# Exponentials in three groups a batch, weight chunks rounded earlier and a busier start, in a fused attention and SwiGLU kernel

## The chip, the cores and the metric

One NeuronCore of a Trainium2 chip runs the whole kernel. The metric is the device time of one execution in microseconds (us), read from several executions. The engines are TensorE (PE, matmuls; PEld is its weight load), VectorE (DVE), ScalarE (ACT), GpSimd (POOL) and SyncE (SP, which issues DMAs). The kernel gives each engine its own list of instructions; where one needs another's result, it waits for a semaphore.

## The reference

```python
# x: (4, 12416, 128), inducing: (32, 128); weights of the FFN are float64
def mab(q, kv):
    s = (q @ kv.transpose(0, 2, 1)) / sqrt(128)
    a = exp(s - s.max(-1, keepdims=True))
    return (a / (a.sum(-1, keepdims=True) + 1e-09)) @ kv
h = mab(inducing, x)            # 32 rows a batch: first softmax, over 12416 columns
y = mab(x, h)                   # second softmax, over 32 columns
xn = y / sqrt(mean(y * y) + 1e-06) * rms_g
g, val = xn @ w_gate, xn @ w_val         # 128 -> 1536
out = (g / (1 + exp(-g)) * val) @ w_out  # silu(g) * val, 1536 -> 128
```

## The kernel before

The FFN is a stream of 1,200 **slots**: 4 batches of 25 units of tokens, each with 12 slots of 128 hidden columns. In a slot PE makes gate and value, ACT makes silu, DVE multiplies the two into `u`, and PE multiplies some earlier `u` by `w_out`. Most of these output products are "plain" (fp32). Some are "split" into three fp32r matmuls, whose operands ACT and POOL make first; `ready` is the slot from which a split product may be issued.

```python
def slot(j, products, steps):
    g = ps_gv.tile([P, 512], F32, name="gv", tag="gv")     # ps_gv: four PSUM banks in turn
    nc.tensor.matmul(g[:, 0:T], sg[:, ts(j, P)], a[:, 0:T], start=True, stop=True)
    sl = silp.tile([P, 512], F32, name="silu")
    nc.scalar.activation(sl[:, 0:T], g[:, 0:T], AF.Silu)
    products()                                             # one or two earlier output products
    v = ps_gv.tile([P, 512], F32, name="gv", tag="gv")
    nc.tensor.matmul(v[:, 0:T], sv[:, ts(j, P)], a[:, 0:T], start=True, stop=True)
    t = up.tile([P, 512], F32, name="u")
    nc.vector.tensor_tensor(out=t[:, 0:T], in0=sl[:, 0:T], in1=v[:, 0:T], op=ALU.mult)
    steps()                                                # this slot's share of the attention
    # ... (u joins the plain or the split products that wait)
```

The attention of the next batch is dealt out over the slots by `steps()`. Its two softmaxes have seven **batches of exponentials** in the stream: one of batch 0 (its second softmax), then two for each later batch. Each is one long instruction on ACT (in batch 0 and in the second softmax a short one follows). A `mark` is its slot. Ahead of a mark, `products()` holds products back, so that PE has a stock of five (`LAG`) to live on:

```python
add(254, g["exp2"], 0, NS)          # in schedule(b)
marks += [134, 254]                 # 134: exp1, the first softmax
# ...
hold = any(k < e <= k + 3 for e in marks)   # in products(), k is the slot
if hold and count < LAG:
    return
```

Two other parts matter. First, x's phase and the start, before slot 0: x comes in seven blocks, PE turns each and makes the scores, then come the first softmax, its sums (`sum_h`), h, and the first tokens' RMS norm. `warm(n)` issues n matmuls whose result nobody reads. Second, the **rounding**: the weights come as float64, in nine chunks, and each is rounded to fp32 from its bits by some seven instructions on DVE, ACT and POOL (`power`, `power_number`, `upper`, `upper_number`, `sign`, `lower`). The early chunks are done before slot 0, the rest in slots 0 to 16, where the stream already needs them.

Last, a **seam** turns one group of attention weights into the FFN's input: transposes on DVE, a power of -0.5 on POOL (`scale`, 2.9 us), its application (`apply`) on POOL, another DVE transpose (`turn_b`), `split`.

Of the kernel before, what the change touches and what calls it, by code (L numbers as in the profile page):

```python
# [18 lines left out]
P = 128  # L19
R = 4  # L20
# [4 lines left out]
def kernel(  # L25
# [109 lines left out]
    def load_rows(b, s):  # L135

        n = per[s]
        t = xnat[b, s] = xnp.tile([P, 16 if b and n > 4 else n, C], F32, name=f"xn{s % 2 if b and n > 4 else s}")
        if b or s == full:
            for q in range(R):  # L140
                nc.sync.dma_start(out=t[ts(q, m), 0:n, :], in_=of(xrows, b, s)[q])
        else:
            d = xrows[ds(start[s], P * n), :].rearrange("(p t) c -> p t c", t=n)
            for t0, t1 in (((0, R), (R, 2 * R), (2 * R, n)) if not s else ((0, n),)):
                nc.sync.dma_start(out=t[:, t0:t1, :], in_=d[:, t0:t1, :])
# [43 lines left out]

    warm(4)  # L190
    ps = ps_m.tile([P, 512], F32, name="mm", tag="mm")
# [27 lines left out]
    def rounding(i, c):  # L219
# [19 lines left out]

        def power(engine=nc.scalar):  # L240
            if i < 2:
                t = w0[i, c] = (silp.tile([P, 512], F32, name="silu") if (i, c) == (1, 0) else
                                 third.tile([P, 512], F32, name="hs") if (i, c) == (1, 1) else
                                 wp.tile([P, 512], F32, name="w"))
                dst = st["dst"] = t[:]
            else:
                dst = st["dst"] = wo.rearrange("p j c -> p (j c)")[:, ts(c, 512)]
            if not wide:
                nc.sync.dma_start(out=dst if i < 2 else dst.rearrange("p (j c) -> p j c", c=C), in_=source(i, c))
                return  # L250
            words = raw[i, c].rearrange("p (f w) -> p f w", w=2)
            st["low"], st["high"] = words[:, :, 0], words[:, :, 1]
            e = st["e"] = work.tile([P, 512], I32, name="we", tag="work")
            nc.vector.tensor_scalar(out=e[:], in0=st["high"], scalar1=20, scalar2=0x7FF,
                                    op0=ALU.logical_shift_right, op1=ALU.bitwise_and)
            if engine is not nc.scalar:
                nc.vector.tensor_scalar(out=e[:], in0=e[:], scalar1=896.0, scalar2=1151.0, op0=ALU.max, op1=ALU.min)

        def power_number(engine=nc.scalar):
            if wide:  # L260
                numbers("e", -896.0 * (1 << 23), float(1 << 23), engine)

# [29 lines left out]
    def attention(b, load_next):  # L292
# [56 lines left out]
        def max3():  # L349
# [4 lines left out]
            nc.vector.tensor_copy(out=nbias[:], in_=ps[:, 0:1])  # L354

        def exp1():
            hl = st["hl"] = once.tile([P, C + 1], F32, name="hl")
            part = sc[b][:, 0:SC1]
            nc.scalar.activation(part, part, AF.Exp, bias=st["nbias"][:], scale=SCALE, accum_out=hl[:, C:C + 1])

# [233 lines left out]
    def ffn(b, u):  # L594
# [59 lines left out]

        def slot(j, products, steps):
            g = ps_gv.tile([P, 512], F32, name="gv", tag="gv")
            nc.tensor.matmul(g[:, 0:T], sg[:, ts(j, P)], a[:, 0:T], start=True, stop=True)  # L657
            sl = silp.tile([P, 512], F32, name="silu")
            nc.scalar.activation(sl[:, 0:T], g[:, 0:T], AF.Silu)  # L659
            products()  # L660
            v = ps_gv.tile([P, 512], F32, name="gv", tag="gv")
            nc.tensor.matmul(v[:, 0:T], sv[:, ts(j, P)], a[:, 0:T], start=True, stop=True)  # L662
            t = up.tile([P, 512], F32, name="u")
            nc.vector.tensor_tensor(out=t[:, 0:T], in0=sl[:, 0:T], in1=v[:, 0:T], op=ALU.mult)  # L664
            steps()
# [10 lines left out]
    for s in range(NS):  # L676
        load_rows(0, s)
        for _ in range(1 if s == 1 else 4 if s == NS - 1 else 0):
            fetch_raw(*unread.pop(0))
    weight = {one: rounding(*one) for one in chunks}  # L680

    def parts(i, c, *engine):
        one = weight[i, c]
        one["power"](*engine)
        one["power_number"](*engine)
        one["upper"]()
        one["upper_number"](*engine)
# [6 lines left out]
    for s in range(NS):  # L694
        for k in range(R):
            f["turn_x"](s, k)
        if s:
            f["scores1"](s - 1)
        if s == 2:
            parts(0, 0, nc.vector)  # L700
        if s == 3:
            join(0, 0)
    f["scores1"](NS - 1)
    f["max1"]()
    warm(4)
    f["max2"]()
    warm(3)
    f["max3"]()
    warm(8)
    f["exp1_of"](0, 1)  # L710
    for s in range(NS):
        if s % 2:
            f["exp1_of"](s, min(s + 2, NS))
        f["turn_e"](s)
        if s == 5:
            parts(1, 0)
        if s == NS - 1:
            f["fold_l"]()
        f["sum_h"](s)
# [3 lines left out]
    f["square_h"]()  # L723
    weight[1, 0]["sign"]()
    f["stack_of"](0, 0)
    warm(10)
    f["scores2"](0, ps)
    f["sub_max"](0)
    weight[1, 0]["lower"]()
    f["exp2"](0, 1)  # L730
# [4 lines left out]
    square()  # L735
    parts(2, 0)
    f["stack_of"](1, 0)
    warm(26)
    turn_z()
    scale()  # L740
    weight[2, 0]["sign"]()
    for i in range(2):
        f["stack_low"](i, 0)
    parts(0, 1)
    apply()
    turn_b()
    split()
    weight[2, 0]["lower"]()
    spread(0, 0)
    warm(3)  # L750
    gather(0, 1)
    gather(0, 2)
    join(0, 1)
    flowing.append(True)
# [5 lines left out]
    def schedule(b):  # L760
# [4 lines left out]
        def add(k, step, *args):  # L765
            plan.setdefault(int(k), []).append(lambda: step(*args))
            if getattr(step, "__name__", "") == "sub_max" and args[0]:
                busy[int(k)] = 1.1

        if not b:  # L770
            for k, one in ((0, (1, 1)), (3, (2, 1)), (7, (0, 2)), (10, (1, 2)), (13, (2, 2))):
                for j, name in ((0, "power"), (1, "power_number"), (1, "upper"), (2, "upper_number"), (2, "sign"), (3, "lower")):
                    add(k + j, weight[one][name])
            for k, *one in ((2, 0, 1), (5, 1, 1), (12, 0, 2), (15, 1, 2)):
                add(k, f["stack_of"], *one)
# [3 lines left out]
            for s in range(1, NS):  # L779
                add(2 * s + 16, f["scores2"], s)  # L780
                add(2 * s + 17, f["sub_max"], s)
            add(3 * NS + 9, f["exp2"], 1, NS)
            marks.append(3 * NS + 9)
        if b + 1 < B:
# [4 lines left out]
            for s in range(NS):  # L789
# [8 lines left out]
                add(203 + 7 * s, g["sub_max"], s)  # L798
            for k, name in ((126, "max1"), (128, "max2"), (130, "max3"), (134, "exp1"), (187, "fold_l"), (189, "divide"), (191, "turn_h"),
                            (193, "square_h")):  # L800
                add(k, g[name])
            for i in range(2):
                add(175 + 23 * i, g["fetch"], i)
                add(197 + 7 * i, g["stack"], i)
                for k in range(R):
                    add(199 + 7 * i + k, g["place"], i, k)
            add(254, g["exp2"], 0, NS)
            marks += [134, 254]
        if b + 2 < B:
# [8 lines left out]
    for k, (b, s) in enumerate(order):  # L818
# [5 lines left out]
        for late_by, one in enumerate(following):  # L824
            for i, step in enumerate(seam(*one)):
# [3 lines left out]
                seams.setdefault(at, []).append(step)  # L829
                seam_busy[at] = seam_busy.get(at, 0) + {3: 3.0, 4: 1.2, 6: 1.4}.get(i, 0)  # L830
    flat = [(b, u) for b in range(B) for u in range(NU)]
    after = dict(zip(flat, flat[1:]))
# [18 lines left out]
    for b in range(B):  # L851
# [6 lines left out]
        for k, (u, j) in enumerate(order):  # L858
# [16 lines left out]
            def products():  # L875
# [3 lines left out]
                count = max(len(plain) - 1, 0) + sum(at <= now for at, _ in kara)  # L879
                hold = any(k < e <= k + 3 for e in marks)  # L880
                if hold and count < LAG:
# [8 lines left out]
            if u not in unit:  # L890
                unit[u] = ffn(b, u)
            unit[u](j, products, steps)
    while kara or plain:
# [33 lines left out]
```

## Time and profile before

| | before |
|---|---|
| time, median of 4 runs | 1690.6 us (1689.47 to 1691.07) |
| start of slot 0 | 55.42 us |
| PE busy share; PE's share of the chain that ended last | 98%; 90% |
| half clock inside the stream | 54.8 to 58.2 us, 126.5 to 129.9 us |
| ACT table loads | 16, of 1.28 us |

PE is nearly always busy, so time can only be won where PE waits, runs at half clock, or does filler. This is the timeline of before around one such wait (start, duration, engine, line, operation, operands; in brackets the idle time just before and what ended it):

```profile
119.72 2.90 POOL L524 TENSOR_TENSOR rs<-ms,mhalf 128x16 f32<-128x16 f32 x1 [0.19 <-DVE ms L522]
...
122.70 1.05 POOL L528 TENSOR_TENSOR sc<-sc,rs 128x512 f32<-128x512 f32 x1
123.70 1.27 POOL L650 TENSOR_TENSOR xn<-hs,u 128x512 fp32r<-128x512 f32 x1
...
125.03 0.50 PE L607 MATMUL acc<-xn,xn 128*128 128x512 f32 x1 [2.68 <-POOL xn L650]
```

The reader is to see a queue on POOL: the power of the first seam, its application, and only then L650, the last step of a split product's operand. PE stands still for 2.68 us until that operand is there.

### The profile page before, as it was taken

What the parts mean: (1) busy time and instruction counts of PE and PEld (TensorE: products, weight loads), DVE (VectorE), ACT (ScalarE), POOL (GpSimd) and SP (SyncE); (2) the same over time, 40 slices, a digit from 0 to 9 for tenths busy, and PEclk for the clock granted to TensorE, in tenths of its full rate; (3) what the DMA queues carried; (4) which work ended last, traced back from release to release, by engine and by line L of the source; (5) the groups of instructions that cost most, each with busy time, mean ns of one, the idle gap of its engine ahead of it and who ended that gap; (6) DMA issues with size and microseconds to landing.
All of it is one profiled execution on the core that took longest, in us unless ns stands there. A gap on an engine that the chain in (4) does not pass through costs nothing.

```text
span 1688.5 us, 23205 instructions
## 1 busy us (share of the span) xinstructions
PE 1660.7 (98%) x6756; PEld 1036.6 (61%) x6756; DVE 1166.2 (69%) x1941; ACT 1237.4 (73%) x2216; POOL 1159.4 (69%) x931
## 2 busy tenths in 40 slices
PE   9989999999999999999999999999999999999998
PEld 6546665655676565665566666565557666666666
DVE  4877775676667776667667777676767666666665
ACT  4547777766787777776778777777677888788786
POOL 0336775777587775776668777577657888888884
PEclk9999999999999999999999999999999999999999
DMA  6445523433444131524335314252211111111111
GB/s 233 106 64 90 86 57 83 101 85 59 68 81 68 37 82 30 124 60 102 60 64 83 58 33 82 51 131 65 50 30 38 30 39 32 38 32 38 31 36 26
DMA packets 389454, 112.38 MB, mean 67 GB/s; under 512 B 365104, under 2 KB 369744, under 8 KB 386896
## 3 DMA queue, kind: packets, MB, share of 16 engines
q1 hardware_dynamic: 389136, 110.89, 32.1%
q8 instruction: 54, 0.88, 0.2%
q14 instruction: 72, 0.59, 0.1%
q10 hardware_dynamic: 192, 0.02, 0.0%
HBM read 53.95 MB, written 27.00 MB: 48 GB/s over the span
## 4 chain that ended last, share of the span: by engine, by line
PE 90%; ACT 2%; issue 1%; POOL 1%; DVE 1%; DVEq 0%; POOLq 0%; ACTq 0%
PE acc L607 42%; PE gv L657 17%; PE gv L662 16%; PE u L625 5%; PE u L623 5%; PE mm L330 3%; PE mm L509 1%; PE mm L388 1%; DVE u L664 1%; ACT silu L659 1%; ACT L659 1%; PE mm L461 0%; ACT L448 0%; POOL xn L650 0%; ACT sc L448 0%
## 5 line engine op out<-in xcount | busy, mean ns | idle before, releaser
L664 DVE TENSOR_TENSOR u<-silu,gv 128x512 f32<-128x512 f32 (+2 forms) x1200 | 788.0, 664 | 470.8 <-PE gv L662 236.0
L659 ACT ACTIVATE silu<-gv 128x512 f32<-128x512 f32 (+2 forms) x1200 | 698.6, 584 | 376.4 <-PE gv L657 340.0
L607 PE MATMUL acc<-u,wo 128*128 128x512 f32 (+2 forms) x1600 | 794.1, 580 | 3.5 <-DVE u L664 2.2
L662 PE MATMUL gv<-a,sv 128*128 128x512 f32 (+2 forms) x1188 | 760.2, 640 | 0.9 <-DVE u L664 0.6
L645 POOL TENSOR_TENSOR xn<-u,xn 128x512 fp32r<-128x512 f32 (+2 forms) x400 | 503.4, 1258 | 366.8 <-ACT xn L644 329.3
L650 POOL TENSOR_TENSOR xn<-hs,u 128x512 fp32r<-128x512 f32 (+2 forms) x400 | 503.6, 1259 | 39.3 <-ACT hs L649 36.1
L657 PE MATMUL gv<-a,sg 128*128 128x512 f32 (+2 forms) x1188 | 486.2, 409 | 6.0 <-ACT silu L659 6.0
L657 PEld LDWEIGHTS gv<-a,sg 128*128 128x128 f32 x1188 | 224.9, 189 | 238.3 <-ACT silu L659 120.6
L607 PEld LDWEIGHTS acc<-u,wo 128*128 128x128 f32 x1600 | 298.6, 189 | 82.6 <-issue 16.4
L662 PEld LDWEIGHTS gv<-a,sv 128*128 128x128 f32 x1188 | 224.7, 189 | 194.5 <-issue 137.7
L644 ACT ACTIVATE xn<-u 128x512 fp32r<-128x512 f32 (+2 forms) x400 | 247.7, 619 | 25.6 <-DVE u L664 23.7
L649 ACT ACTIVATE hs<-xn 128x512 f32<-128x512 f32 (+2 forms) x400 | 245.8, 614 | 4.9 <-POOL xn L650 4.0
L607 PE MATMUL acc<-xn,xn 128*128 128x512 f32 (+2 forms) x400 | 156.5, 391 | 4.5 <-POOL xn L650 4.5
L625 PE MATMUL u<-xn,xn 128*128 128x512 f32 (+2 forms) x400 | 155.7, 389 | 0.0
L623 PE MATMUL u<-xn,xn 128*128 128x512 f32 (+2 forms) x400 | 155.3, 388 | 0.0
L607 PEld LDWEIGHTS acc<-xn,xn 128*128 128x128 f32 x400 | 75.0, 188 | 24.2 <-POOL xn L650 7.6
L524 POOL TENSOR_TENSOR rs<-ms,mhalf 128x16 f32<-128x16 f32 (+2 forms) x28 | 75.9, 2709 | 16.9 <-DVE ms L522 15.1
L625 PEld LDWEIGHTS u<-xn,xn 128*128 128x128 f32 x400 | 75.2, 188 | 18.1
L623 PEld LDWEIGHTS u<-xn,xn 128*128 128x128 f32 x400 | 75.1, 188 | 16.8 <-issue 0.7
L616 DVE STREAM_TRANSPOSE o<-o 128x512 f32<-128x512 f32 (+2 forms) x97 | 67.7, 698 | 3.4
L615 DVE TENSOR_TENSOR o<-acc,o 128x512 f32<-128x512 f32 (+2 forms) x97 | 64.9, 669 | 0.0
L628 ACT ACTIVATE o<-u 128x512 f32<-128x512 f32 (+2 forms) x97 | 56.4, 582 | 0.0
(165 smaller groups left out, 745.1 us busy)
## 6 DMA issues: line engine op xcount, KB each, us to landing
out_dram<-o SPq DMA_DIRECT2D x320, 64.0 KB, 1.9
xn<-in_x_dram SPq DMA_DIRECT2D x62, 256.0 KB, 4.8
xT<-in_x_dram SPq DMA_DIRECT2D x60, 256.0 KB, 5.4
a<-hi SPq DMA_DIRECT2D x156, 64.0 KB, 2.0
a<-lo SPq DMA_DIRECT2D x156, 64.0 KB, 2.0
w<-w SPq DMA_DIRECT2D x22, 256.0 KB, 3.1
xn<-in_x_dram SPq DMA_DIRECT2D x4, 1024.0 KB, 10.9
out_dram<-o SPq DMA_DIRECT2D x64, 60.0 KB, 1.9
```

The costliest lines, as they stand in the source:

```text
L524: nc.gpsimd.tensor_tensor(out=rs, in0=ms, in1=mhalf[rows, 0:n], op=ALU.pow)
L607: nc.tensor.matmul(acc[:, 0:T], lhsT, rhs, start=st["left"] == NJ, stop=st["left"] == 1)
L623: nc.tensor.matmul(ups[:, 0:T], w[:, i, :], hi, start=st["k"] == nk, stop=False)
L625: nc.tensor.matmul(ups[:, 0:T], w[:, NK + i, :], lo, start=False, stop=not st["k"])
L644: nc.scalar.activation(hi, v, AF.Copy, scale=1.0 - 2.0 ** -13)
L645: nc.gpsimd.tensor_tensor(out=lo, in0=v, in1=hi.bitcast(F32), op=ALU.subtract)
L649: nc.scalar.activation(hs[:, 0:T], hi.bitcast(F32), AF.Copy, scale=1.0 + 2.0 ** -12)
L650: nc.gpsimd.tensor_tensor(out=d, in0=hs[:, 0:T], in1=v, op=ALU.subtract)
L657: nc.tensor.matmul(g[:, 0:T], sg[:, ts(j, P)], a[:, 0:T], start=True, stop=True)
L659: nc.scalar.activation(sl[:, 0:T], g[:, 0:T], AF.Silu)
L662: nc.tensor.matmul(v[:, 0:T], sv[:, ts(j, P)], a[:, 0:T], start=True, stop=True)
L664: nc.vector.tensor_tensor(out=t[:, 0:T], in0=sl[:, 0:T], in1=v[:, 0:T], op=ALU.mult)
```

## The change

The intent: (1) slice each batch of exponentials into three groups over three slots, and let the two slots after the first make silu as (tanh(g/2)+1)*g/2, so that the silu table isn't needed between the groups; start the hold two slots ahead, not three. (2) Round the weight chunks sooner: chunk (1,0) (first index: 0 gate, 1 value, 2 output weights), in the shadow of the first softmax, and the later ones moved up behind it. (3) In x's phase, give PE more filler before and within x's first block, load x's second block (and its sixth) in two parts, and load the first weight chunk after x's third block, not its second. The diff, cut to its core:

```diff
-            for t0, t1 in (((0, R), (R, 2 * R), (2 * R, n)) if not s else ((0, n),)):
+            for t0, t1 in (((0, R), (R, 2 * R), (2 * R, n)) if not s else ((0, 2 * R), (2 * R, n)) if s in (1, full - 1) else ((0, n),)):
                 nc.sync.dma_start(out=t[:, t0:t1, :], in_=d[:, t0:t1, :])
-    warm(4)
+    warm(6)
... (the bound on the exponent moves from power to power_number; exp1 is dropped)
-        def slot(j, products, steps):
+        def slot(j, products, steps, tanh):
             g = ps_gv.tile([P, 512], F32, name="gv", tag="gv")
             nc.tensor.matmul(g[:, 0:T], sg[:, ts(j, P)], a[:, 0:T], start=True, stop=True)
             sl = silp.tile([P, 512], F32, name="silu")
-            nc.scalar.activation(sl[:, 0:T], g[:, 0:T], AF.Silu)
+            if tanh:
+                nc.scalar.activation(sl[:, 0:T], g[:, 0:T], AF.Tanh, scale=0.5)
+                nc.vector.scalar_tensor_tensor(out=sl[:, 0:T], in0=sl[:, 0:T], scalar=1.0, in1=g[:, 0:T],
+                                               op0=ALU.add, op1=ALU.mult)
+            else:
+                nc.scalar.activation(sl[:, 0:T], g[:, 0:T], AF.Silu)
...
-            nc.vector.tensor_tensor(out=t[:, 0:T], in0=sl[:, 0:T], in1=v[:, 0:T], op=ALU.mult)
+            if tanh:
+                nc.vector.scalar_tensor_tensor(out=t[:, 0:T], in0=sl[:, 0:T], scalar=0.5, in1=v[:, 0:T],
+                                               op0=ALU.mult, op1=ALU.mult)
+            else: ... (as before)
...
-        for _ in range(1 if s == 1 else 4 if s == NS - 1 else 0):
+        for _ in range(1 if s == 2 else 4 if s == NS - 1 else 0):
             fetch_raw(*unread.pop(0))
...
             f["turn_x"](s, k)
+            if not s and k < 2:
+                warm(1)
...
+    one = weight[1, 0]
     f["max1"]()
+    one["power"]()
     warm(4)
     f["max2"]()
+    one["upper"]()
... (power_number after max3)
         f["turn_e"](s)
-        if s == 5:
-            parts(1, 0)
+        if not s:
+            one["upper_number"](nc.vector)
+        if s == 1:
+            one["sign"]()
+        if s == 2:
+            one["lower"]()
+        if s == NS - 1:
+            parts(2, 0)
... (chunks (2,0), (0,1) and (1,1) move up likewise; chunk (0,0) waits one block of x longer)
+        def exponentials(k, step, first):
+            groups = list(range(first, NS - 1, 2))
+            for i, s in enumerate(groups):
+                add(k + i, step, s, NS if s == groups[-1] else s + 2)
+                if i:
+                    by_tanh.add((b, k + i))
+            return k
...
-            for k, one in ((0, (1, 1)), (3, (2, 1)), (7, (0, 2)), (10, (1, 2)), (13, (2, 2))):
+            add(0, weight[1, 1]["sign"])
+            add(1, weight[1, 1]["lower"])
+            for k, one in ((1, (2, 1)), (5, (0, 2)), (8, (1, 2)), (11, (2, 2))):
...
-            add(254, g["exp2"], 0, NS)
-            marks += [134, 254]
+            marks += [exponentials(134, g["exp1_of"], 0), exponentials(254, g["exp2"], 0)]
...
-                hold = any(k < e <= k + 3 for e in marks)
+                hold = any(k < e <= k + 2 for e in marks)
```

More of the change, by code (lines that the diff above doesn't have):

```diff
@@ L238, in numbers, with power @@
                 engine.tensor_scalar(out=to[:], in0=t[:], scalar1=mul, scalar2=add, op0=ALU.mult, op1=ALU.add)
-        def power(engine=nc.scalar):
+        def power():
             if i < 2:
@@ L255, in power @@
                                     op0=ALU.logical_shift_right, op1=ALU.bitwise_and)
-            if engine is not nc.scalar:
-                nc.vector.tensor_scalar(out=e[:], in0=e[:], scalar1=896.0, scalar2=1151.0, op0=ALU.max, op1=ALU.min)
         def power_number(engine=nc.scalar):
             if wide:
+                e = st["e"]
+                if engine is not nc.scalar:
+                    nc.vector.tensor_scalar(out=e[:], in0=e[:], scalar1=896.0, scalar2=1151.0, op0=ALU.max, op1=ALU.min)
                 numbers("e", -896.0 * (1 << 23), float(1 << 23), engine)
@@ L354, in max3 @@
             nc.vector.tensor_copy(out=nbias[:], in_=ps[:, 0:1])
-        def exp1():
-            hl = st["hl"] = once.tile([P, C + 1], F32, name="hl")
-            part = sc[b][:, 0:SC1]
-            nc.scalar.activation(part, part, AF.Exp, bias=st["nbias"][:], scale=SCALE, accum_out=hl[:, C:C + 1])
         def exp1_of(s0, s1):
@@ L663, in slot @@
             t = up.tile([P, 512], F32, name="u")
-            nc.vector.tensor_tensor(out=t[:, 0:T], in0=sl[:, 0:T], in1=v[:, 0:T], op=ALU.mult)
+            if tanh:
+                nc.vector.scalar_tensor_tensor(out=t[:, 0:T], in0=sl[:, 0:T], scalar=0.5, in1=v[:, 0:T],
+                                               op0=ALU.mult, op1=ALU.mult)
+            else:
+                nc.vector.tensor_tensor(out=t[:, 0:T], in0=sl[:, 0:T], in1=v[:, 0:T], op=ALU.mult)
             steps()
@@ L683, in parts @@
         one = weight[i, c]
-        one["power"](*engine)
+        one["power"]()
         one["power_number"](*engine)
@@ L696 @@
             f["turn_x"](s, k)
+            if not s and k < 2:
+                warm(1)
         if s:
             f["scores1"](s - 1)
-        if s == 2:
+        if s == 3:
             parts(0, 0, nc.vector)
-        if s == 3:
+        if s == 4:
             join(0, 0)
     f["scores1"](NS - 1)
+    one = weight[1, 0]
     f["max1"]()
+    one["power"]()
     warm(4)
     f["max2"]()
+    one["upper"]()
     warm(3)
     f["max3"]()
+    one["power_number"](nc.vector)
     warm(8)
@@ L723 @@
     f["square_h"]()
-    weight[1, 0]["sign"]()
+    weight[2, 0]["sign"]()
     f["stack_of"](0, 0)
@@ L728 @@
     f["sub_max"](0)
-    weight[1, 0]["lower"]()
+    weight[2, 0]["lower"]()
     f["exp2"](0, 1)
@@ L735 @@
     square()
-    parts(2, 0)
+    parts(0, 1)
     f["stack_of"](1, 0)
@@ L740 @@
     scale()
-    weight[2, 0]["sign"]()
+    weight[0, 1]["sign"]()
     for i in range(2):
         f["stack_low"](i, 0)
-    parts(0, 1)
+    parts(1, 1)
     apply()
@@ L747 @@
     split()
-    weight[2, 0]["lower"]()
     spread(0, 0)
@@ L752 @@
     gather(0, 2)
-    join(0, 1)
+    weight[0, 1]["lower"]()
     flowing.append(True)
@@ L768, in add @@
                 busy[int(k)] = 1.1
+        def exponentials(k, step, first):
[5 more added lines that the diff above has]
+            return k
         if not b:
-            for k, one in ((0, (1, 1)), (3, (2, 1)), (7, (0, 2)), (10, (1, 2)), (13, (2, 2))):
+            add(0, weight[1, 1]["sign"])
+            add(1, weight[1, 1]["lower"])
+            for k, one in ((1, (2, 1)), (5, (0, 2)), (8, (1, 2)), (11, (2, 2))):
                 for j, name in ((0, "power"), (1, "power_number"), (1, "upper"), (2, "upper_number"), (2, "sign"), (3, "lower")):
                     add(k + j, weight[one][name])
-            for k, *one in ((2, 0, 1), (5, 1, 1), (12, 0, 2), (15, 1, 2)):
+            for k, *one in ((2, 0, 1), (4, 1, 1), (11, 0, 2), (13, 1, 2)):
                 add(k, f["stack_of"], *one)
@@ L781, in schedule @@
                 add(2 * s + 17, f["sub_max"], s)
-            add(3 * NS + 9, f["exp2"], 1, NS)
-            marks.append(3 * NS + 9)
+            marks.append(exponentials(3 * NS + 9, f["exp2"], 1))
         if b + 1 < B:
@@ L798, in schedule @@
                 add(203 + 7 * s, g["sub_max"], s)
-            for k, name in ((126, "max1"), (128, "max2"), (130, "max3"), (134, "exp1"), (187, "fold_l"), (189, "divide"), (191, "turn_h"),
+            for k, name in ((126, "max1"), (128, "max2"), (130, "max3"), (187, "fold_l"), (189, "divide"), (191, "turn_h"),
                             (193, "square_h")):
@@ L830 @@
                 seam_busy[at] = seam_busy.get(at, 0) + {3: 3.0, 4: 1.2, 6: 1.4}.get(i, 0)
+    by_tanh = set()
     flat = [(b, u) for b in range(B) for u in range(NU)]
@@ L891 @@
                 unit[u] = ffn(b, u)
-            unit[u](j, products, steps)
+            unit[u](j, products, steps, (b, k) in by_tanh)
     while kara or plain:
```

## The prediction

> **What bounds the kernel now.** I read the page's busy line first, then its chain of work that ended last.
>
> ```profile
> PE 1660.7 (98%) x6756; PEld 1036.6 (61%) x6756; DVE 1166.2 (69%) x1941; ACT 1237.4 (73%) x2216; POOL 1159.4 (69%) x931
> ...
> PE 90%; ACT 2%; issue 1%; POOL 1%; DVE 1%; DVEq 0%; POOLq 0%; ACTq 0%
> ```
>
> TensorE (PE) is busy for 98% and is 90% of the chain. So a change that removes no matmul can win only the places where PE stands still or does filler: the start, before the first slot at 55.4 us (gate matmul, line L657), and stalls in the stream of 1,200 slots after it. A plain slot costs PE 1.33 us when nothing holds it (gate to gate in the timeline, for example 67.24 to 68.57). To find the stalls I took every step from one matmul's start to the next, and subtracted the usual step for the same sequence of lines. The first place is where ScalarE (ACT) does a batch of exponentials, seven times. One of them in the timeline, ACT and PE (start, duration, engine, line; in brackets the idle time before and what ended it):
>
> ```profile
> 257.37 1.28 ACT L359 ACT_TABLE_LOAD   x1
> 258.67 2.88 ACT L359 ACTIVATE sc<-sc,nbias 128x3104 f32<-128x3104 f32 x1
> 261.66 1.28 ACT L659 ACT_TABLE_LOAD   x1
> 262.24 0.80 PE L662 MATMUL gv<-a,sv 128*128 128x512 f32 x1
> 262.95 1.78 ACT L659 ACTIVATE silu<-gv 128x512 f32<-128x512 f32 x3
> 263.60 0.49 PE L657 MATMUL gv<-a,sg 128*128 128x512 f32 x1 [0.57 <-ACT silu L659]
> 264.33 1.13 PE L607 MATMUL acc<-u,wo 128*128 128x512 f32 x2 [0.23 <-DVE u L664]
> ```
>
> For 5.6 us (257.37 to 262.95) there is no silu. PE lives on saved-up output products, two a slot (L607, some 0.86 us each), until the four PSUM banks of gate and value are full; then it waits. The excess over the usual steps is 0.73 + 0.49 + 0.61 us (the last at 265.76), **1.83 us**, at each of three first exponentials (near 262, 671, 1080). At the three second ones (near 437, 846, 1255) it is 1.13 + 0.47 = **1.60 us**. At batch 0's (near 112) it is 0.40 + 0.49 = 0.89. Sum: 3 x 1.83 + 3 x 1.60 + 0.89 = **11.2 us**.
>
> The second place is the weights' rounding, early in the stream:
>
> ```profile
> 64.95 1.12 PE L475 MATMUL mm<-hs,hg 128*128 128x512 f32 x2 [0.70 <-POOL hs L283]
> ...
> 83.64 0.50 PE L662 MATMUL gv<-a,sv 128*128 128x512 f32 x1 [0.31 <-DVE sv L480]
> ...
> 86.93 1.13 PE L607 MATMUL acc<-u,wo 128*128 128x512 f32 x2 [1.24 <-POOL wo L283]
> ```
>
> Against the usual 0.64, 0.03 and 0.23 us of such steps, PE loses 0.86 (at 63.45), 0.51 (74.58), 0.42 (80.05), 0.88 (82.73) and 1.40 (85.30): **4.1 us**, all waits for a chunk rounded too late. VectorE (DVE) is the reason: 14.03 us busy of the 15 between 60 and 75.
>
> The third is x's phase:
>
> ```profile
> 9.59 3.65 PE L321 MATMUL gv<-ident,xn 128*128 128x128 f32 x16 [0.62 <-ACT xT L324]
> 13.17 1.38 PE L330 MATMUL gv<-xT,indT 128*32 128x512 f32 x8
> 14.49 1.97 PE L321 MATMUL gv<-ident,xn 128*128 128x128 f32 x16
> ```
>
> Sixteen transposes take 3.65 us before 13.9 us and 1.97 after, so the array ran slow until then. The second block of x lands at 9.46 in the trace's landings, which is when PE starts on it. Later blocks land at 13.21, 15.71, 18.21 and 20.98, each 1 to 2 us before PE comes to them (14.49, 17.38, 20.27, 23.17): from there PE sets the pace, 2.89 us a block.
>
> **What the Trainium skill says.** "TensorE: Matmul & The Clock Gate", Part 1, has the array at half clock by default and after a mostly idle window of 3413 ns, at full clock after a busy one. The trace agrees: the granted clock is 0.71, 0.50 and 0.94 in 54-56, 56-58 and 58-60 us, together 3.4 us at half, after PE idled 1.7 us around 53; it also fits the slow transposes. "ScalarE: Activation LUTs", "Table sets: the hidden batching unit", lists tanh with exp, so tanh between exponentials needs no load; silu does. "What ACT_TABLE_LOAD costs" gives 1283 ns for the load, as here (7 loads, mean 1283), but another 1380 for a drain. Here the load starts 0.01 us after silu's end and exp 0.02 after the load, so a switch costs 1.3 us. "VectorE: DVE Perf Modes", "Why PSUM operands drop a tier", has fp32 with a PSUM operand at one element a cycle: the product u from PSUM takes 664 ns, and SCALAR_TENSOR_TENSOR from SBUF 682, so I take 0.69 us for each new one.
>
> **The change, part by part.** (1) Exponentials. Both table loads stay, 2 x 1.28, and the exponentials stay some 3 us plus 0.4 for two more starts. New: the two slots within have tanh (0.6 us, as silu) and two DVE operations of 0.69 for one, 1.4 us in a slot in which PE needs 2.2. I lay out one case in us from the end of the last silu, slot e:
> - ACT: load to 1.3; exponentials 1.3-2.5; tanh of e+1 to 3.1; exponentials to 4.2; tanh of e+2 to 4.9; exponentials to 6.1; load to 7.4; silu of e+3 to 8.0, of e+4 to 9.0.
> - PE, two products a slot, 2.18 us: gate of e+1 at 1.3, e+2 at 3.5, e+3 at 5.7, e+4 at 7.9, e+5 at 9.2.
> - DVE: u of e+1 at 4.5, e+2 at 6.6, e+3 at 8.7.
>
> The bank that the gate of e+5 needs is free at 8.0, and every product finds its u ready, so PE doesn't wait. The narrower hold (two slots, not three) puts the full stock of five products at slot e; before, two were spent one slot earlier. I expect the 11.2 us to come back nearly whole and take **10.3**, 0.1 to 0.15 being left at each.
>
> (2) Rounding. Three chunks move out of the early stream or forward: the stream no longer has one chunk's sign and lower (0.69 + 0.68) nor another's two masks (2 x 0.43) on DVE, 2.2 us, and the last chunks come two slots (2.7 us) sooner. The waits of 0.86, 0.51, 0.88 and 1.40 are all shorter than that. The 0.42 at 80.05 stays in part, since between that chunk's end and its use there are still two slots. **3.4** of 4.1 us.
>
> (3) x's phase. x's second block is loaded in halves, so its first half should land near 8.3. Filler matmuls warm the array one or two windows sooner, and the third block goes ahead of the weights and lands near 12.0 instead of 13.2. Then blocks are at hand at 15.7 and 18.2: the fourth runs 15.7 to 18.6, the fifth 18.6 to 21.5, and the sixth starts at 21.5 instead of 23.17. **1.7 us** gained; landings now set part of the pace, so a warmer array can't give more.
>
> (4) What this costs. The chunk taken into the softmax of x puts two operations of 0.69 and 0.68 on DVE between the transposes of the exponentials, in 32 to 35 us. PE needs 0.86 us for each block's sums, DVE then 1.35 for operation and transpose, twice: 2 x 0.49, **1.0 us lost**. Its five operations around the maximum (0.43 each) fit in waits of DVE that are there already (0.45, 0.47 and 0.88 us).
>
> Between 37 and 55 us the chain (power on POOL, 3.29 us, then apply, transposes and split) is unchanged. Sum: 10.3 + 3.4 + 1.7 - 1.0 = **14.4 us**; 1690.9 - 14.4 = 1676.5.
>
> **The rivals.** A: PE waits just as long, later. Total ACT work at a batch of exponentials grows by 0.4 us and DVE's by 1.4; if the backlog only moves to slots e+3 to e+5, half is lost: gain some 9 us in all, 1682. Against it: ACT is 73% and DVE 69% busy, and my layout has slack of over 1 us at e+5. B: a different wait takes over. After batch 0's exponentials PE stands for 2.85 us at 121.95, for a product whose POOL step (L650) is queued behind the power and its apply; it is in the same order after. I count no gain from it. If its slots shift against POOL by a microsecond it could give or take 1 to 2 us, the more so as the array then falls to half clock for a window (0.63 and 0.52 in 126-130): 1.6 us. C: the start gains nothing, since the loads and the 3.29 us power decide, and DVE's new work delays the sums: 0.7 us less. D: tanh makes the compiler load another table at each group: four loads more each time, 7 x 5.1 us of ACT, and PE slower by perhaps 15 us. The skill's list speaks against it.
>
> **Range and chances.** Full recovery of all the waits gives 11.2 + 4.1 + 1.7 = 17, and luck with the clock window 2 more: 1672. Half of (1) and nothing at the start gives 1682 to 1683. I take 1671 to 1683. Faster by over 2% would need 33.8 us, more than everything that PE waits for in these places; slower by over 2% would need D twice over. So within 2% is nearly certain: 0.98.
>
> **What would show it.** Table loads: still 15 or 16 in all. Tanh 14 times (two in each of seven), with 28 new DVE operations of near 0.69 us. At each batch of exponentials the excess of PE's steps falls from 1.6-1.8 to under 0.3 us; if it is over 0.8, A is right. Between 60 and 90 us at most one wait for rounding of over 0.4 us remains. x's sixth block of transposes starts near 21.5, full clock comes before 11 us, and the sums end with DVE as the last wait. The first slot starts near 54.7 (55.4 before). The 2.85 us wait near 120 is still there. It would be wrong if loads rise (D), if the first slot doesn't come sooner (C), or if the 120 us stall vanishes or doubles (B).

## The result, and the profile after

| | before | after |
|---|---|---|
| time, median of 4 runs each | 1690.6 us (1689.47 to 1691.07) | 1675.07 us (1673.44 to 1675.7) |
| start of slot 0 in the profiled run | 55.42 us | 55.29 us |
| ACT table loads | 16 | 16 |
| half clock inside the stream | 54.8 to 58.2, 126.5 to 129.9 us | 55.6 to 59.0, 120.4 to 123.8 us |

The ratio is 0.9908, with a 95% interval of 0.989 to 0.9925. A ratio is the mean time of one kernel's runs over that of the other's of the same rounds, so not quite the ratio of the medians. The gain is clear of noise, and within 2%.

First the page of after: the busy line of its part 1, and the engines' shares of the chain that ended last.

```profile
PE 1653.8 (99%) x6764; PEld 1034.8 (62%) x6764; DVE 1175.4 (70%) x1961; ACT 1237.5 (74%) x2234; POOL 1160.3 (69%) x931
...
PE 96%; DVE 1%; POOL 1%; DMA 1%; ACT 0%; issue 0%; SPq 0%; DVEq 0%; POOLq 0%
```

The chain has 96% of PE where it had 90%. PE's busy time fell by 6.9 us, although it has eight matmuls more. Of these, 1.8 us lie before 55 us (47.3 us busy there, 49.1 in before), where x's transposes run at full clock sooner; I didn't follow the others.

**A batch of exponentials**, the first one after slot 134, in the timeline of after:

```profile
252.09 1.28 ACT L364 ACT_TABLE_LOAD   x1
...
253.38 1.15 ACT L364 ACTIVATE sc<-sc,nbias 128x1024 f32<-128x1024 f32 x1
...
254.53 0.58 ACT L657 ACTIVATE silu<-gv 128x512 f32<-128x512 f32 x1
...
255.00 1.14 ACT L364 ACTIVATE sc<-sc,nbias 128x1024 f32<-128x1024 f32 x1
255.13 0.69 DVE L658 SCALAR_TENSOR_TENSOR silu<-silu,gv 128x512 f32<-128x512 f32 x1 [0.96 <-ACT silu L657]
...
256.14 0.58 ACT L657 ACTIVATE silu<-gv 128x512 f32<-128x512 f32 x1
...
256.62 1.17 ACT L364 ACTIVATE sc<-sc,nbias 128x1056 f32<-128x1056 f32 x1
...
257.89 1.28 ACT L661 ACT_TABLE_LOAD   x1
...
259.19 0.60 ACT L661 ACTIVATE silu<-gv 128x512 f32<-128x512 f32 x1
...
259.77 0.40 PE L653 MATMUL gv<-a,sg 128*128 128x512 f32 x1
```

Read ACT down the column: table, group, tanh (L657), group, tanh, group, table, silu (L661). There is no table load between a group and a tanh. The gate of the next slot (L653, the last line) has no bracket: PE didn't wait for it. In before there were three waits here. The groups view of after has the new work, with its mean in ns after the comma:

```profile
L667 DVE SCALAR_TENSOR_TENSOR u<-silu,gv 128x512 f32<-128x512 f32 (+1 forms) x14 | 9.4, 674 | 1.5
...
L658 DVE SCALAR_TENSOR_TENSOR silu<-silu,gv 128x512 f32<-128x512 f32 (+1 forms) x14 | 9.2, 657 | 7.0 <-ACT silu L657 7.0
```

The prediction had 0.69 us for each.

**x's phase**, from the timeline of after, PE's transposes (L322) of the second block's second half and of the third, fourth and sixth block:

```profile
10.82 1.06 PE L322 MATMUL gv<-ident,xn 128*128 128x128 f32 x8 [0.20 <-ACT xT L325]
...
13.34 1.94 PE L322 MATMUL gv<-ident,xn 128*128 128x128 f32 x16 [0.46 <-DMA xn<-in_x_dram]
...
17.09 1.94 PE L322 MATMUL gv<-ident,xn 128*128 128x128 f32 x16 [0.81 <-DMA xn<-in_x_dram]
...
22.84 1.86 PE L322 MATMUL gv<-ident,xn 128*128 128x128 f32 x15
```

Sixteen transposes take 1.94 us from the third block on, and eight take 1.06 in the second: the array is at full clock from 4.4 us on, where before it was from 13.9. This is read from the transposes themselves, which follow each other every 0.21 us before these times and every 0.11 after them; the windows view says 1.00 for the granted clock all through these first microseconds, so it doesn't show this slow start. But the third and fourth blocks begin after waits (0.46 and 0.81 us) for the DMA that brings x. The sixth block, the last line, starts at 22.84, only 0.33 us sooner than before.

**The stall near 120 us** is still there:

```profile
115.16 2.91 POOL L520 TENSOR_TENSOR rs<-ms,mhalf 128x16 f32<-128x16 f32 x1 [0.18 <-DVE ms L518]
...
118.14 1.05 POOL L524 TENSOR_TENSOR sc<-sc,rs 128x512 f32<-128x512 f32 x1
119.15 1.27 POOL L646 TENSOR_TENSOR xn<-hs,u 128x512 fp32r<-128x512 f32 x1
...
120.47 0.79 PE L603 MATMUL acc<-xn,xn 128*128 128x512 f32 x1 [2.69 <-POOL xn L646]
```

It is the same queue on POOL, and PE waits 2.69 us. The windows view of after (us of each stretch; busy time and instructions of each engine; PEclk is the granted clock) shows what the wait brings with it: half clock from 120.4 on, for 3.4 us.

```profile
121.00:123.00 2.00, 2.00 (x6) 1.23 (x4) 1.32 (x3) 0.60 (x1) 0.95 (x1) 0.50 0.13 33
123.00:125.00 2.00, 2.00 (x6) 0.97 (x5) 1.49 (x3) 0.60 (x1) 0.00 (x0) 0.79 0.40 98
```

**Where the time went.** I compared the start of the gate matmul of the same slot in both traces. The difference is what has been saved until there:

| saved against before, us, profiled runs | slot 0 | 20 | 34 | 45 | 145 | 265 | 445 | 865 | end |
|---|---|---|---|---|---|---|---|---|---|
| after | 0.13 | 4.14 | 4.56 | 4.59 | 6.36 | 8.10 | 9.86 | 15.10 | 14.56 |

Each step of the table is a place: the start (to slot 0), the rounding (0 to 20), batch 0's exponentials (to 34), the stall (34 to 45), a first softmax (to 145), a second (to 265), and so on. Between the places the column stays flat, so nothing is given back there. About 0.5 us is lost after the last batch of exponentials, in the last 300 slots; that varies between runs from 0 to 0.5, and I didn't follow it.

### The profile page after: what moved, and what is told of

Same layout as the page of the kernel before. It is cut to its first block, busy times and chain, and to the rows that moved or that the text cites. A ratio compares the mean times of both kernels' runs of the same rounds, so it can differ in the third digit from the quotient of the medians.

```text
span 1673.9 us, 23254 instructions
## 1 busy us (share of the span) xinstructions
PE 1653.8 (99%) x6764; PEld 1034.8 (62%) x6764; DVE 1175.4 (70%) x1961; ACT 1237.5 (74%) x2234; POOL 1160.3 (69%) x931
## 4 chain that ended last, share of the span: by engine, by line
PE 96%; DVE 1%; POOL 1%; DMA 1%; ACT 0%; issue 0%; SPq 0%; DVEq 0%; POOLq 0%
PE acc L603 45%; PE gv L653 17%; PE gv L664 16%; PE u L621 5%; PE u L619 5%; PE mm L331 3%; PE mm L505 1%; PE mm L384 1%; DMA xn<-in_x_dram 1%; POOL rs L520 0%; PE gv L322 0%; PE mm L457 0%; DVE u L670 0%; PE gv L331 0%; POOL xn L646 0%
## 5 line engine op out<-in xcount | busy, mean ns | idle before, releaser
L670 DVE TENSOR_TENSOR u<-silu,gv 128x512 f32<-128x512 f32 (+2 forms) x1186 | 779.9, 664 | 442.0 <-PE gv L664 228.0
L661 ACT ACTIVATE silu<-gv 128x512 f32<-128x512 f32 (+2 forms) x1186 | 691.9, 584 | 362.8 <-PE gv L653 326.6
L653 PE MATMUL gv<-a,sg 128*128 128x512 f32 (+2 forms) x1188 | 484.3, 408 | 0.0
L653 PEld LDWEIGHTS gv<-a,sg 128*128 128x128 f32 x1188 | 224.6, 189 | 228.7 <-ACT silu L661 110.5
```

## The experiments

Each profiled run is read by the same table. All results were right. The ratios are against before, in the same rounds on the same chip.

| saved, us | slot 0 | 20 | 34 | 45 | 145 | 265 | 445 | 865 | end |
|---|---|---|---|---|---|---|---|---|---|
| exp_only | -0.35 | -0.39 | 0.04 | 1.66 | 3.43 | 5.17 | 6.59 | 11.78 | 11.43 |
| no_exp | 1.09 | 5.08 | 5.07 | 5.27 | 5.28 | 5.26 | 5.22 | 5.22 | 5.05 |
| single_hold2 | 0.97 | 5.83 | 4.96 | 4.94 | 5.91 | 5.81 | 6.73 | 7.51 | 7.34 |
| hold3 | 0.46 | 5.34 | 6.11 | 7.75 | 9.05 | 10.74 | 12.01 | 16.64 | 16.11 |
| silu_between | 1.26 | 6.12 | 2.92 | 2.57 | -3.69 | -9.49 | -15.01 | -31.18 | -31.24 |
| old_loads | 0.58 | 5.46 | 5.88 | 5.95 | 7.71 | 9.43 | 11.18 | 16.44 | 16.27 |
| no_warm | 0.41 | 5.26 | 5.69 | 5.70 | 7.48 | 9.21 | 10.94 | 16.20 | 15.66 |
| late_sign | -0.46 | 3.54 | 3.96 | 4.04 | 5.81 | 7.53 | 9.29 | 14.56 | 14.04 |
| later_product | 0.12 | 5.00 | 5.42 | 6.18 | 7.96 | 9.69 | 11.44 | 16.70 | 16.19 |
| early_seam | 0.99 | 5.85 | 6.05 | 11.09 | 12.86 | 14.58 | 15.95 | 21.16 | 21.01 |
| early_seam_old_loads | 0.31 | 5.18 | 5.38 | 10.43 | 12.20 | 13.95 | 15.67 | 20.94 | 20.60 |

### The exponentials alone, and all but the exponentials

`exp_only` is before with the new `slot`, `exponentials` and hold; `no_exp` is after with one group a batch and the old hold:

```diff
 def exponentials(k, step, first):
-    groups = list(range(first, NS - 1, 2))
-    ... (three groups, the last two in tanh slots)
+    add(k, step, first, NS)
     return k
-hold = any(k < e <= k + 2 for e in marks)
+hold = any(k < e <= k + 3 for e in marks)
```

> The kernel before plus part (1) alone: exponentials in three groups, tanh in the two slots between, hold of two slots. My theory: the seven batches give back the same 10.9 us that the slot anchors show in the changed kernel (0.4 + 3 x 1.8 + 3 x 1.7), so 1690.6 - 10.9 = 1679.7 us, 1679 to 1681; first slot still near 55.4, the waits for rounding at slots 3 to 20 still there. Rival (the parts need each other: the earlier rounding frees VectorE for the new operations): clearly less, 1683 or more.

> The changed kernel with part (1) undone: one exponential a batch, silu everywhere, hold of three slots; loads of x, warm-up and earlier rounding stay. My theory: loses the 10.9 us again, 1675.1 + 10.9 = 1686.0, 1685 to 1687; excess at each batch of exponentials 1.6 to 1.8 us as before. Rival (the start or the rounding made more of the gain): under 1684.

Measured: exp_only 1679.0 us, ratio 0.9933 (0.9918 to 0.9948); no_exp 1684.92 us, ratio 0.9971 (0.9956 to 0.9986), with runs from 1683.17 to 1688.56. In the table exp_only gains in every step that a batch of exponentials ends (0.43 at batch 0, then 1.71 to 1.78; the 1.42 to slot 445 is 1.77 less 0.35 that this run and early_seam lose near slot 296, which I didn't follow) and nothing from 0 to 20; no_exp gains nothing after slot 20 but 0.2 us. The parts are separate: the ratios' shortfalls, 0.67% and 0.29%, sum to 0.96% against after's 0.92%. The time of exp_only is as expected; no_exp lies just under its range of 1685 to 1687 and above the rival's 1684.

### Is it the tanh, the slices or the hold?

`single_hold2` has one group a batch, as no_exp, but the new hold. `hold3` is after with the old hold. `silu_between` is after with silu in the two slots between the groups:

```diff
 # silu_between, against after
     add(k + i, step, s, NS if s == groups[-1] else s + 2)
-    if i:
-        by_tanh.add((b, k + i))
```

> The changed kernel with one exponential a batch and silu everywhere, but with the hold of two slots kept. Rival to be tested: the stock of products, placed one slot later, is what removes the waits, and tanh does little: 1676 to 1679. My theory: the four PSUM banks end PE's work whatever the stock, so the first wait of 0.7 to 1.1 us at each batch stays and only the second one (0.5 us, for a product's u) can go: 1682 to 1685.

> The changed kernel with its three groups of exponentials, but silu instead of tanh in the two slots between, so ScalarE loads tables six times a batch and not twice (four more, 1.28 us each). My theory (ScalarE's uninterrupted block is what PE waits for): from the last silu to the fourth after it 3 x (1.28 + 1.13 + 1.28 + 0.6) = 12.9 us, against some 8 us of PE work at hand, so 4 to 5 us of wait at each of seven: 1700 to 1710. Rival (smaller groups alone are enough, the loads hide beside PE): under 1680.

> The changed kernel with the hold of three slots again, so the stock of five products is reached a slot earlier and two are spent before the exponentials. My theory: with tanh between, a stock of four is enough or nearly: at most 0.5 us lost at each of the six later batches, 1675 to 1678 us. Rival (tanh helps only with the full stock): 1 us and more at each, 1681 or more.

Measured: single_hold2 1682.53 us, ratio 0.9953 (0.9936 to 0.9969). The hold alone wins 0.93 to 0.96 us at a first softmax, loses 0.1 at a second and 0.87 at batch 0, so the time is in the range that I expected, and the rival's 1676 to 1679 is out. hold3: 1674.82 us, ratio 0.991 (0.9895 to 0.9925). With slices and tanh in place, the old hold costs 0.48 us at a first softmax and 0.05 at a second. At batch 0 it is better by 0.35. (Expected were at most 0.5 at each later batch.) So the slices with tanh recover most of the waits by themselves, and the new hold is worth 3 x 0.48 + 3 x 0.05 - 0.35 = 1.2 us, too little for the medians to show beside the runs' spread.

silu_between: 1723.42 us, ratio 1.0197 (1.0182 to 1.0212), so slices without tanh are worse than no slices. Expected was 1700 to 1710: the direction was right, the size too small. Its timeline at the first exponentials after slot 134:

```profile
261.12 1.28 ACT L661 ACT_TABLE_LOAD   x1
...
263.03 1.28 ACT L364 ACT_TABLE_LOAD   x1
...
263.06 0.50 PE L653 MATMUL gv<-a,sg 128*128 128x512 f32 x1 [1.11 <-ACT silu L661]
...
267.55 0.79 PE L653 MATMUL gv<-a,sg 128*128 128x512 f32 x1 [3.27 <-ACT silu L661]
```

Here every group and every silu has a load of its own (44 in the whole run, not 16), and PE runs out of stock: it waits 1.11 and then 3.27 us for silu. What I had left out is what the second wait does to the clock, in the windows view of the same run:

```profile
266.00:268.00 2.00, 0.45 (x1) 0.45 (x2) 0.47 (x1) 1.97 (x3) 0.00 (x0) 0.63 0.00 0
268.00:270.00 2.00, 2.00 (x4) 0.87 (x4) 0.81 (x2) 1.63 (x3) 1.04 (x1) 0.50 0.00 0
```

Half clock holds from 266.5 to 273.3 us, two windows of 3.4 us, and so at each of the six later batches. They lose 5.3 to 6.3 us each.

### The start

`old_loads` is after with before's order and sizes of the loads. `no_warm` is after without the new filler. `late_sign` does two DVE operations of chunk (1,0) after the last transpose of exponentials, not between the first ones:

```diff
 # old_loads
-    ... else ((0, 2 * R), (2 * R, n)) if s in (1, full - 1) else ((0, n),)
+    ... else ((0, n),)
-    for _ in range(1 if s == 2 else 4 if s == NS - 1 else 0):
+    for _ in range(1 if s == 1 else 4 if s == NS - 1 else 0):
 # no_warm
-    warm(6)
+    warm(4)
-            if not s and k < 2:
-                warm(1)
 # late_sign
-        if s == 1:
-            one["sign"]()
-        if s == 2:
-            one["lower"]()
         if s == NS - 1:
+            one["sign"]()
+            one["lower"]()
             parts(2, 0)
```

> The changed kernel with the loads of x and of the first weight chunk in their former order and pieces, warm-up filler kept. My theory: two things held x's phase, the cold array and the landings, and either cure alone gives most of the 1.5 us, since from the third block on PE's 2.89 us a block decides: sixth block of transposes starts near 22.1 (21.7 to 22.0 in the three runs with both cures, 23.2 to 23.6 with none). Rival (the order of loads made the gain): 23 or later. Time within 1 us of the changed kernel.

> The changed kernel without the added filler matmuls (four at the beginning, none in the first block), loads in the new order. My theory: the second block starts near 8.6 at half clock and the third near 13.5 instead of 12.4, sixth near 22.3; 0.4 us lost, not 1.5. Rival (the warm array made the gain): sixth block at 23 or later. Time within 1 us of the changed kernel.

> The changed kernel with the sign and the lower half of the chunk (1, 0) after the last transpose of exponentials, not between the first ones. My theory: PE's sums wait for VectorE between transposes, so from the first sum to the transpose of h 6.75 us as in the kernel before, not 7.38; first slot 0.6 us sooner for the same landings. Rival (the sums are slower for another reason, or the work comes back as a wait at the reciprocal): 7.2 or more, nothing gained.

Measured: 1673.58 us (ratio 0.9901, 0.9887 to 0.9916), 1674.32 us (0.9908, 0.9893 to 0.9922) and 1673.77 us (0.9905, 0.9891 to 0.992). No interval tells any of the three from the whole change, so the verdicts on the start come from one trace of each. In old_loads the sixth block of transposes starts at 22.43 us (expected near 22.1, the rival's 23 or later), in no_warm at 22.57 (expected near 22.3).

In the traces the landing of x's second block is the largest term, and it differs between kernels whose loads are alike. In the runs with the new loads its first half landed between 8.29 us (silu_between) and 10.35 us (late_sign), and the sixth block started between 21.72 and 23.76 us. In every run with the new loads the sixth block starts 12.12 to 12.17 us after the whole second block has landed, with the filler or without it. So the filler gains nothing there: PE waits for the landings of later blocks anyway. With the old loads the same distance is 13.71 us in before and 13.80 in exp_only (array at half clock), and 12.59 and 12.71 in old_loads and early_seam_old_loads (array warm): the new loads take 1.6 us off it, the filler alone 1.0 to 1.2. But the new loads also come with later landings: the whole second block landed at 9.46 to 9.98 us in the four runs with the old loads and at 9.55 to 11.61 in the nine with the new ones. Whether cutting the block in two makes it later was not tested. In all, the sixth block starts at 22.43 and 22.69 with the filler alone, 22.57 with the loads alone, 22.45 on average with both, and 23.17 and 23.56 with neither. So **filler and new loads cure the same loss**, and either alone gives nearly all of it, as far as one or two traces of each can show. Over the eight profiled runs that have both, slot 0 is at 54.85 us on average (54.17 to 55.89), against 55.6 in the two that have neither: 0.75 us.

The sums took 7.38 us in the changed kernels and 6.75 in before, counted from their first matmul to h's turn. In late_sign they took 7.06, so about half of what I expected (6.75) came; the rival had 7.2 or more. The delayed transposes are indeed cured there, and another operation is delayed in their place. In the timeline of late_sign:

```profile
37.12 1.39 POOL L284 TENSOR_TENSOR silu<-o,we 128x512 f32<-128x512 f32 x1 [9.96 <-DVE o L282]
37.30 1.50 DVE L267 TENSOR_SCALAR o<-sc 128x512 int32<-128x512 int32 x1
```

and the same DVE operation in the timeline of after:

```profile
36.38 0.42 DVE L267 TENSOR_SCALAR o<-sc 128x512 int32<-128x512 int32 x1
```

The mask L267 takes 0.42 us where POOL is idle, and 1.50 where POOL multiplies two SBUF operands at the same time: it ends 0.29 us after POOL does. The Trainium skill, "SBUF — State Buffer", section "SBUF: two separate sides", says that the two engines share a pair of ports as an exclusive lock, for DVE operations of certain modes, and that the loser blocks for the whole instruction. This run agrees, though the trace doesn't name the mask's mode, and this is one pair of instructions. The reciprocal of the sums stands behind the mask on DVE, so it came late.

### The stall near 120 us

Two attempts. `later_product` lets the split product that PE waits for fall due three slots later. `early_seam` moves the first seam's steps: all up to the power and its application a slot sooner, the transpose after them one slot later.

```diff
 # later_product
-    ready[b, u, j] = int((free + 0.3) / SLOT) + 1
+    ready[b, u, j] = int((free + 0.3) / SLOT) + (4 if not b and k == marks[0] + 3 else 1)
 # early_seam
-    j = (... if k else (32, 33, 33, 34, 34, 36, 38))[i]
+    j = (... if k else (31, 32, 32, 33, 33, 37, 38))[i]
```

> The changed kernel with the one split product that PE stands 2.7 us for near 117 us (slot 33's) due three slots later. My theory: the wait is only one of order, plain products are at hand, and GpSimd has finished by then: the 2.7 us go, and with them the half-clock window after it (1.6 us, where it falls), 1670.8 to 1672.5 us; slots 38 to 45 up to 4.3 us sooner. Rival (PE then waits for the next thing that GpSimd's power delays, as the attention weights of the next unit): under 1.5 us gained, and a wait of over 1 us within ten slots.

> The changed kernel with batch 0's first seam one slot earlier up to the apply (31, 32, 32, 33, 33 for turn, square, product, power, apply) and its second turn one slot later (37): possible now that the first group of exponentials is done by slot 31. My theory: the 2.7 us wait near 117 comes from GpSimd's power starting at 115.2 (3.6 slots late), and VectorE's second turn waiting for it in its turn; started some 1.5 to 2 us earlier, both waits shrink to under 1 us and the half-clock window after them mostly goes: slots 38 to 45 2 to 4 us sooner, 1671 to 1673 us. Rival (VectorE is too full in these slots, so the power starts no earlier): under 0.7 us gained there.

> The same with the loads of x in the former order as well. My theory: the order of loads makes no difference beyond the spread of landings, so within 1.0 us of early_seam. Rival (more DMAs in flight delay each block): 1 us or more faster.

Measured: later_product 1673.19 us, ratio 0.9897 (0.9881 to 0.9914). My theory of 1670.8 to 1672.5 missed. In the timeline of later_product:

```profile
118.36 0.71 DVE L528 STREAM_TRANSPOSE aT<-sc 128x512 f32<-128x512 f32 x1 [2.74 <-POOL sc L524]
...
119.70 1.75 PE L603 MATMUL acc<-u,wo 128*128 128x512 f32 x2 [1.92 <-DVE u L670]
```

The split product is gone from the place, and PE waits all the same: 1.92 us for a `u` from DVE, and DVE had stood 2.74 us in front of the seam's transpose, which needs the same POOL power and its application. The wait moved to another engine's queue, as the rival had it. Between slots 34 and 45 it saves 0.76 us, against 0.03 in after.

early_seam: 1669.76 us (1669.25 to 1670.33), ratio 0.988 (0.9863 to 0.9896), better than the 1671 to 1673 that I expected. Its timeline, POOL alone:

```profile
112.02 2.90 POOL L520 TENSOR_TENSOR rs<-ms,mhalf 128x16 f32<-128x16 f32 x1 [7.85 <-DVE ms L518]
...
115.00 1.05 POOL L524 TENSOR_TENSOR sc<-sc,rs 128x512 f32<-128x512 f32 x1
```

The power starts 3.1 us sooner than in after, of which 1.5 are this run's lead at slot 34 (6.05 against 4.56). PE hardly waits there (0.08 us), and the mean granted clock of the run is 1.000. From slot 34 to 45 the run saves 5.04 us where after saves 0.03: 2.7 are the wait, some 1.6 are the half clock (exp_only and hold3, in whose profiled runs the wait brought no half-clock window, save 1.62 and 1.64 there), and 0.7 I didn't follow. The edit does three things at once: the power and the steps ahead of it start sooner, the transpose waits one slot longer, and slot 33's product is planned as plain. Which of the three is needed stays open.

early_seam_old_loads, with the old loads as well: 1669.81 us, ratio 0.9882 (0.9867 to 0.9897), the same as early_seam. As expected, the order of the loads makes no difference that these runs can show once the filler is there. **early_seam is faster than both kernels**: than after by 5.3 us of the medians, measured in other rounds, but no run of the one reaches the times of the other, and the traces show where the time went.

## Why the prediction was right or wrong

Predicted were 1676.5 us (1671 to 1683) and a gain of 14.4; measured were 1675.07 and 15.5 by the medians, 14.6 in the profiled pair. It was within 2%, as predicted with 0.98.

- **(1) Exponentials: right, slightly under-sized.** 10.3 us were predicted; the seven steps of after sum to 0.42 + 3 x 1.77 + 3 x 1.73 = 10.9. The marks at the later batches gave back nearly all (1.77 of 1.83; 1.73 where 1.60 had been counted). Batch 0's gave less: 0.42 of 0.89, because PE waits 0.40 us there for a transpose on DVE, a wait that before doesn't have; in hold3 it is 0.08 us, so it comes with the shorter hold. no_exp shows that nothing else gives these microseconds, hold3 that slices and tanh do most of it.
- **(2) Rounding: right.** 3.4 predicted, 4.0 measured. All five waits are gone, the one at 80 us too, which I had left in part.
- **(3) x's phase: the term that was mis-sized.** The step said "its first half should land near 8.3", and with it 1.7 us. In the profiled run it landed at 9.42 and the sixth block gained 0.33; over the eight runs the sixth block gained 0.9 (23.37 in the two without the change, 22.45 in the eight). I had read the landing of one trace as if it belonged to the program. It moves by 2 us between runs, and the new loads may be part of that (see above). In the four runs in which it landed at 8.29 to 8.62, the sixth block started at 21.72 to 22.00, near the 21.5 predicted: the mechanism was right, and so was the remark that landings then set the pace.
- **(4) The sums: right in mechanism, 0.64 us lost, not 1.0.** And from h's turn to the power, 9.31 us took the place of 9.73, a gain of 0.42 that I hadn't foreseen; its cause wasn't tested (it is the same in all eleven kernels with the new rounding, and absent in exp_only). Start in all: 0.7 predicted, 0.13 in the profiled run, 0.75 on average.
- **Rivals.** A (the backlog moves on) is refuted: at slots e+3 to e+5 no step of PE is over 0.2 us longer than usual. D (more table loads) is refuted: 16 loads in both; silu_between has D's four further loads at each of the seven, and is 33 us slower than before by the medians, not the 15 I had given it. C (the start gains nothing) holds for the profiled run alone. B: the stall stayed, 2.69 us of waiting for 2.68 (the prediction's 2.85 is the step's excess over the usual, 2.86 in after), which is what I counted on.
- **The spread.** Runs of after differ by up to 2 us. Among the profiled runs of the eleven kernels with the new rounding, the half-clock window at the start of the stream appears in three (after, no_exp, late_sign). Those save 4.0 us from slot 0 to 20, the others 4.85 to 4.88, so that window costs 0.86 us. It comes and goes in kernels that are alike there. The window after the stall is absent in exp_only, hold3 and silu_between, which have the same wait of 2.69 us, and costs 1.6. The traces show what this hangs on. In one run the changes of the clock lie on one grid: in before 54.8 and 126.5 us are 71.7 apart, 21 times 3.413 us, and 13.9, where full clock began, is 12 times before 54.8; in after 55.6 and 120.4 are 19 times apart, and 4.4 is 15 times before 55.6. Where the grid lies differs from run to run. Near the stall, PE stood still for 56 to 78% of one interval of this grid in the eight profiled runs where half clock followed; in the three where it didn't, the wait fell over two intervals (37 and 41% in exp_only, 41 and 38% in hold3, 51 and 28% in silu_between). So the window is luck of the run, and to end the wait, as in early_seam, is what the program can do. (Before slot 0 idle shares of 41 and 42% went both ways, so no threshold follows.)

## What to carry to other kernels

When a long instruction blocks an engine that feeds the bound one, slice it so that each slice fits in the stock of the bound engine, and put between the slices only work that needs no new table: slices that each cost two table loads are worse than none. To find the end of a stall, follow the queue of the engine that is late back to the instruction that starts it. Giving the last waiter more time only passed the wait to the next one in line; starting the head of the queue sooner, together with what else early_seam moved, removed it. And compare several traces before a DMA's landing, or a window of half clock, is booked as a gain of the program.

## What the Trainium skill lacked or had wrong

- "ScalarE: Activation LUTs", "What ACT_TABLE_LOAD costs": the 1283 ns of the load agree, but the further 1380 ns for a drain do not show: in after a load starts at 252.09 and the exponential follows at 253.38, 1.29 us later. Counted with the page's sum, each switch would look twice as dear as it is here.
- No page that I read says which table set silu is in. Here it is not that of exp: silu between the groups adds loads (44 in silu_between), where tanh adds none (16 in both kernels), as "ScalarE: Activation LUTs", "Table sets: the hidden batching unit", has it for tanh.
- "TensorE: Matmul & The Clock Gate", Part 1, agrees on the 3.4 us of a window and on its running freely, not in step with the kernel (71.7 us is 21 times 3.413). How idle a window has to be it doesn't say: here a PE wait of 2.69 us, less than a window, brought half clock where 66 to 78% of one window (57% in before) was idle, and not in exp_only, hold3 and silu_between. The price of one in this stream is 0.86 to 1.6 us.
- "TensorE: Matmul & The Clock Gate", Part 4, "PE-mode transpose", says that full clock doesn't engage in transpose mode. In before PE did transposes by the identity from 9.59 to 13.2 us and then scores, and the clock was full from 13.9 us; in after the transposes themselves follow each other every 0.11 us, not every 0.21, from 4.4 us on. The trace calls them plain matmuls, so whether they are in that mode it doesn't show; if they are, it disagrees.
- "SBUF — State Buffer", "SBUF: two separate sides", has the loser of the lock blocked for the whole instruction. The mask beside the POOL multiplication took 1.50 us but ended only 0.29 us after it, less than the 0.42 that it takes alone; times on POOL are rough, so this is no clear contradiction.
- No page that I read gives the spread of a DMA's landing between runs. The same load, the first half of x's second block, landed between 8.29 and 10.35 us in nine runs.
